# Attention backward for one query row: the score and grad products with the query standing and the keys moving

## The chip, the cores and the metric

The kernel runs on one core of a Trainium2 chip. The metric is device time in microseconds for one launch, the median of several runs. TensorE multiplies matrices (one operand stands in its array, the other moves through it) and writes PSUM; VectorE and ScalarE read and write PSUM and SBUF; SyncE and ScalarE issue the DMAs here. In the profile these are PE (PEld for its weight loads), DVE, ACT and SP.

## What is computed

For 2 x 32 = 64 heads, each with one query row of 128 and 8192 keys and values of 128, all in bf16: the output of softmax attention and the gradients of q, k and v for a given `grad_out`.

```python
def _fwd_reference(q, k, v):
    scale = q.shape[-1] ** -0.5
    scores = jnp.einsum("bhqd,bhkd->bhqk", q, k) * scale
    p = _softmax(scores, axis=-1)
    return jnp.einsum("bhqk,bhkd->bhqd", p, v)

def reference(q, k, v, grad_out):
    ...
    _out, _vjp = jax.vjp(_f, q, k, v)
    _grads = _vjp(grad_out)
    ...
```

With P = softmax(scale q k^T), dP = grad_out v^T and delta = sum(P dP): out = P v; dS = P (dP - delta); dq = scale dS k; dk is the outer product of scale dS and q; dv that of P and grad_out. Each head reads 4 MB (k, v) and writes 4 MB (dk, dv).

## The kernel before

A head's k is one SBUF tile `kt` of 128 partitions x 64 rows x 128 elements, its v another, `vt`; each is one DMA of 2 MB (`load`, L96). There are five buffers of each (`UNITS`). The gradients dv and dk are written in place over `vt` and `kt` and stored from there by ScalarE's queue (`store`, L277), so a load of head h+3 waits until the store of head h-2 has landed.

Scores and dP need k and v with the 128 elements on the partitions. A head is cut into eight steps j, four over k and four over v, each of two halves u of eight 128x128 blocks. `transposes` (L105) turns the eight blocks on TensorE by matmuls against the identity into `tp`, a PSUM tile of two banks of which there are two; ScalarE copies it to `ev` as bf16, VectorE does so for u=1 of j=0 and j=7 (L116). One half-step later in each group, `products` (L123) multiplies the blocks of the step before: each transposed block stands, and one column, q or grad_out of the head, moves, so that each block of 128 keys gives one column of 128 in `sm` (scores) or `dp`. Of step j=7, products follow in the next head's j=0.

Softmax for head h, called y in the loop, follows in its own pass: `row_max` (VectorE) after j=4, `all_max` at j=5 (a transpose on TensorE, then VectorE's `gm`), `exps` at j=6 (a matmul that spreads the maximum, VectorE's `negm`, ScalarE's exponential to `E`), and `to_weights` at the end of j=7, which puts E as bf16 columns into `wz`, the zero-padded weights of `weighted_rows`. The rest of a head p = h-1, called x, runs in the next head's pass: `deltas` (VectorE) after j=0, `sums` (TensorE) at j=1, `weights` (seven small VectorE instructions) after j=1, `weighted_rows` in j=0 to 3 (four concurrent matmuls with 32 standing columns and 512 moving each: out at j=0 and 1, dq at 2 and 3), eight `outer` products on VectorE in j=1 to 6, the store of v after j=4 and of k after j=7. Every fourth head the accumulator is copied out (`acc_to_sbuf`, after j=4) and `combine` (after j=6) picks four heads' rows into columns by f32 matmuls in a PSUM tile `c`; `spread_rows` copies q and grad_out of four heads to all partitions after j=7.

The order is written out by hand: `tc.manual_schedule()` (L298) keeps each engine's instructions in the order in which the loop emits them, and an engine that waits holds all behind it. So TensorE's order within a half-step is transposes, then what stands under `u == 0`, then products, then weighted rows; VectorE's and ScalarE's follow from the calls behind them.

[...]

Of the kernel before, what the change touches and what calls it, by code (L numbers as in the profile page):

```python
# [22 lines left out]
def kernel(  # L23
# [34 lines left out]
    for g in range(1, 4):  # L58
        nc.vector.tensor_add(out=pick[:], in0=pick[:], in1=idv[:, g])

    q_rows = q.rearrange("b h s d -> (b h s) d")
    do_rows = grad_out.rearrange("b h s d -> (b h s) d")
    o_rows = out_0.rearrange("b h s d -> (b h s) d")
# [16 lines left out]
    qT_all = const.tile([P, BH], BF16)  # L80
    doT_all = const.tile([P, BH], BF16)


    rl_all = const.tile([P, 2, BH], F32)
# [20 lines left out]
    def transposes(h, j, u):  # L105
# [14 lines left out]
        x.ev = getattr(x, "ev", {})  # L120
        x.ev[j, u] = ev

    def products(h, j, u):  # L123
        x = heads[h]
        w, c = divmod(j, NS // 2)
        if c == 0 and u == 0:
            if w:
                x.dp = ps_one.tile([P, NT + 2], F32, name="dp", tag="dp")
            else:
                x.sm = ps_one.tile([P, NT + P + 1], F32, name="sm", tag="sm")  # L130
        ev = x.ev.pop((j, u))
        col = (qT_all, doT_all)[w][:, h : h + 1]
        for i in range(HC):
            n = c * CH + u * HC + i
            nc.tensor.matmul(  # L135
                (x.dp if w else x.sm)[:, n : n + 1], lhsT=ev[:, i, :], rhs=col,
                start=True, stop=True,
            )

    def spread_rows(g):  # L140

# [14 lines left out]

    def row_max(x):
        x.mp = work.tile([P, 1], F32, name="mp", tag="mp")
        nc.vector.reduce_max(out=x.mp[:], in_=x.sm[:, 0:NT], axis=AX.X)  # L159

    def all_max(x):
        mT = x.sm[0:1, NT : NT + P]
        nc.tensor.transpose(mT, x.mp[:], ident_f[:])  # L163
        x.gm = work.tile([1, 1], F32, name="gm", tag="gm")
        nc.vector.reduce_max(out=x.gm[:], in_=mT, axis=AX.X)

    def exps(x):
        mb = x.sm[:, NT + P : NT + P + 1]
        nc.tensor.matmul(mb, lhsT=ones_f[0:1, :], rhs=x.gm[:], start=True, stop=True)  # L169
        negm = work.tile([P, 1], F32, name="negm", tag="negm")  # L170
        nc.vector.tensor_scalar(out=negm[:], in0=mb, scalar1=-scale, scalar2=None, op0=ALU.mult)  # L171
        x.E = work.tile([P, NT], F32, name="E_f", tag="E_f")
        x.ld = work.tile([P, 2], F32, name="ld", tag="ld")
        nc.scalar.activation(  # L174
            out=x.E[:],
            in_=x.sm[:, 0:NT],
            func=ACT.Exp,
            bias=negm[:],
            scale=scale,
            accum_out=x.ld[:, 0:1],  # L180
        )
# [8 lines left out]
    def deltas(x):  # L190
        junk = work.tile([P, NT], BF16, name="junk", tag="junk")
        nc.vector.tensor_tensor_reduce(  # L192
            out=junk[:],
            in0=x.E[:],
            in1=x.dp[:, 0:NT],
            scale=1.0,
            scalar=0.0,
            op0=ALU.mult,
            op1=ALU.add,
            accum_out=x.ld[:, 1:2],  # L200
        )

    def sums(x):
        x.lsum = x.dp[:, NT : NT + 2]
        nc.tensor.matmul(x.lsum, lhsT=ones_f[:], rhs=x.ld[:], start=True, stop=True)  # L205

    def weights(h):
        x = heads[h]
        rl, rls = rl_all[:, 0, h : h + 1], rl_all[:, 1, h : h + 1]
        nc.vector.reciprocal(out=rl, in_=x.lsum[:, 0:1])  # L210
        negdelta = work.tile([P, 1], F32, name="negdelta", tag="negdelta")
        nc.vector.tensor_scalar(
            out=negdelta[:], in0=x.lsum[:, 1:2], scalar1=rl, scalar2=-1.0,
            op0=ALU.mult, op1=ALU.mult,
        )
        nc.vector.tensor_scalar(out=rls, in0=rl, scalar1=scale, scalar2=None, op0=ALU.mult)
        dSu = work.tile([P, NT], F32, name="dSu", tag="dSu")
        nc.vector.scalar_tensor_tensor(
            out=dSu[:], in0=x.dp[:, 0:NT], scalar=negdelta[:], in1=x.E[:],
            op0=ALU.add, op1=ALU.mult,  # L220
        )
# [31 lines left out]
    def combine(h):  # L253

        x = heads[h]
        c = ps_one.tile([P, 2, OG], F32, name="c", tag="c")
        for j in range(4):
            nc.tensor.matmul(  # L258
                c[:], lhsT=x.accsb[:, j * D : (j + 1) * D], rhs=pick[:, j],
                start=(j == 0), stop=(j == 3),  # L260
            )
        own = slice(h - OG + 1, h + 1)
        nc.vector.tensor_mul(out=colsT[:, :, own], in0=c[:], in1=rl_all[:, :, own])
# [26 lines left out]
    for w in range(2):  # L290
        for t in wz[w]:
            nc.gpsimd.memset(t[:], 0.0)
    for src, dst in ((nat[:, 0, :], qT_all), (nat[:, 1, :], doT_all)):
        tps = ps_tp.tile([P, BH], BF16, name="tps", tag="tp")
        nc.tensor.transpose(tps[:], src, ident_bf[:BH, :BH])
        nc.vector.tensor_copy(out=dst[:], in_=tps[:])

    with tc.manual_schedule():  # L298
        for h in range(min(UNITS, BH)):
            load(h)  # L300
        for h in range(BH + 1):
# [4 lines left out]
            for j in range(NS):  # L306
                for u in range(2):
                    if y:
                        transposes(h, j, u)
                    if u == 0:  # L310
                        if x and j == 1:
                            sums(x)
                        if y and j == 5:
                            all_max(y)
                        if y and j == 6:
                            exps(y)
                    if y and j:
                        products(h, j - 1, u)
                    elif x and j == 0:
                        products(p, NS - 1, u)  # L320
                    if x and j < 4:
                        weighted_rows(p, j // 2, (2 * (j % 2) + u,))
                if x and j == 0:
                    deltas(x)
                if x and j == 1:
                    weights(p)
                if y and j == 4:
                    row_max(y)
                if y and j == 7:
# [51 lines left out]
```

## Time and profile before

| what | value |
|---|---|
| median of three runs | 1304.23 us (1302.53 to 1307.31) |
| the profiled execution | 1302.89 us |
| its span in the profile | 1301.1 us |
| mean granted TensorE clock | 0.885 |
| busy PE, PEld, DVE, ACT | 85%, 70%, 68%, 70% of the span |
| HBM traffic | 413 GB/s over the span |
| L135, all old products | PE busy 178.9 + 178.6 us, x8192; weight loads 332.4 us |
| L240, weighted rows | PE busy 124.3 + 108.2 us, x2048; mean of one 476 and 415 ns |
| L258, combine's matmuls, 128x128 standing, 8 moving, f32 | x128, 264 ns mean of one |
| L119, ScalarE's copy of `tp` | x896, 1025 ns |
| L270, outer products on VectorE | x512, 1212 and 1216 ns |
| L251, VectorE's copy 128x512 f32 from PSUM | x16, 683 ns |

Busy time of a group is the union of its instructions, so four concurrent matmuls of 415 ns count once. Where instructions of one engine overlap at their ends, the spacing of starts is shorter than the duration of one: four outer products in a row took 4.62 us.

### The profile page before, as it was taken

Reading aid. Unit: us, or ns where it says so; the run is one execution under the profiler, and the core shown is the slowest. Engines: PE = TensorE matmul, PEld = TensorE weight load, DVE = VectorE, ACT = ScalarE, POOL = GpSimd, SP = SyncE. Lnnn points to the kernel's source line nnn. Section 1 sums busy time; section 2 is a strip of 40 time slices with the busy share of each in tenths; the row PEclk is TensorE's granted clock in tenths of the full one; section 3 lists DMA queues with packets and bytes.
Section 4 is the critical chain, followed back from the end, with each engine's and each line's share of the span. In section 5 each row is a group of like instructions: output and inputs, shape, how many; then the busy total and the mean of one; then the engine's idle time right before and its main releaser. Section 6 shows DMA issues by size and latency. Waiting matters only on the chain.

```text
span 1301.1 us, 42243 instructions
## 1 busy us (share of the span) xinstructions
PE 1108.2 (85%) x18948; PEld 911.0 (70%) x18948; DVE 887.4 (68%) x1511; ACT 906.3 (70%) x1043; POOL 4.8 (0%) x16
## 2 busy tenths in 40 slices
PE   5999998988889879898898888988889888888784
PEld 5777777766767667677776767767767677677673
DVE  2887777766766767667676676766667667676566
ACT  5887778867767767676776766766668576676562
POOL 1000000000000000000000000000000000000000
PEclk9999989889887998888898888888899888898786
DMA  9999999999999999999999999999999999999986
GB/s 396 418 427 427 426 428 426 428 427 429 427 428 426 426 419 421 421 427 421 418 421 421 426 421 418 421 408 421 416 418 417 411 425 419 413 412 421 391 356 268
DMA packets 37653, 539.65 MB, mean 415 GB/s; under 512 B 4448, under 2 KB 4448, under 8 KB 4448
## 3 DMA queue, kind: packets, MB, share of 16 engines
q1 hardware_dynamic: 18432, 268.44, 49.6%
q10 hardware_dynamic: 19040, 268.51, 48.7%
q8 instruction: 148, 2.42, 0.7%
q14 instruction: 33, 0.27, 0.1%
HBM read 268.47 MB, written 268.47 MB: 413 GB/s over the span
## 4 chain that ended last, share of the span: by engine, by line
DMA 76%; PE 10%; ACT 6%; issue 4%; DVE 3%; ACTq 0%; DVEq 0%; SPq 0%
DMA out_dram<-kt 74%; PE tp L112 6%; ACT ev L119 5%; DVE ev L117 2%; PE acc L240 2%; DMA kt<-in_k_dram 1%; PE sm L135 1%; DMA nat<-in_grad_out_dram 1%; PE dp L205 0%; DVE kt L270 0%; DVE vt L270 0%; PE dp L135 0%; ACT E_f L174 0%; PE c L258 0%; PE sm L163 0%
## 5 line engine op out<-in xcount | busy, mean ns | idle before, releaser
L119 ACT CAST ev<-tp 128x1024 bf16<-128x1024 f32 x896 | 879.8, 1025 | 326.7 <-PE tp L112 270.7
L112 PE MATMUL tp<-ident_bf,kt 128*128 128x128 bf16 x4096 | 375.8, 245 | 83.3 <-DMA kt<-in_k_dram 54.8
L112 PEld LDWEIGHTS <-kt 128*128 128x128 bf16 x4096 | 281.1, 110 | 218.0 <-issue 156.4
L112 PE MATMUL tp<-ident_bf,vt 128*128 128x128 bf16 x4096 | 316.7, 221 | 60.4 <-ACT ev L119 44.3
L135 PEld LDWEIGHTS <-ev 128*128 128x128 bf16 x8192 | 332.4, 100 | 2.1 <-issue 0.2
L112 PEld LDWEIGHTS <-vt 128*128 128x128 bf16 x4096 | 260.9, 98 | 94.6 <-issue 74.2
L117 DVE CAST ev<-tp 128x1024 bf16<-128x1024 f32 x128 | 156.7, 1224 | 246.0 <-PE tp L112 237.3
L270 DVE TENSOR_TENSOR kt<-qd,dS 128x2048 bf16<-128x2048 bf16 x256 | 310.0, 1212 | 0.0
L270 DVE TENSOR_TENSOR vt<-qd,P 128x2048 bf16<-128x2048 bf16 x256 | 295.8, 1216 | 0.0
L135 PE MATMUL dp<-doT_all,ev 128*128 128x1 bf16 x4096 | 178.9, 165 | 0.1
L135 PE MATMUL sm<-qT_all,ev 128*128 128x1 bf16 x4096 | 178.6, 164 | 0.0
L240 PE MATMUL acc<-vt,wz 128*32 128x512 bf16 x1024 | 124.3, 476 | 9.3 <-DVE wz L185 9.2
L240 PE MATMUL acc<-kt,wz 128*32 128x512 bf16 x1024 | 108.2, 415 | 0.4 <-DVE wz L185 0.4
L240 PEld LDWEIGHTS <-wz 128*32 128x32 bf16 x2048 | 53.6, 95 | 21.7 <-DVE wz L185 12.4
L159 DVE TENSOR_REDUCE mp<-sm 128x1 f32<-128x64 f32 x64 | 14.4, 225 | 74.3 <-PE sm L135 74.3
L153 ACT CAST qd<-pb 128x1024 bf16<-128x1024 f32 x16 | 16.2, 1012 | 43.4 <-DMA out_dram<-kt 39.6
L210 DVE RECIPROCAL rl_all<-dp 128x1 f32<-128x1 f32 x64 | 10.8, 168 | 39.6 <-PE dp L205 39.6
L205 PE MATMUL dp<-ld,ones_f 128*128 128x2 f32 x128 | 28.4, 291 | 8.8 <-DVE ld L192 8.6
L205 PEld LDWEIGHTS dp<-ld,ones_f 128*128 128x128 f32 x128 | 24.8, 242 | 14.1 <-DVE ld L192 13.5
L171 DVE TENSOR_SCALAR negm<-sm 128x1 f32<-128x1 f32 x64 | 9.9, 154 | 23.9 <-PE sm L169 23.9
L169 PE MATMUL sm<-gm,ones_f 1*128 1x1 f32 x128 | 24.4, 257 | 0.0
L169 PEld LDWEIGHTS sm<-gm,ones_f 1*128 1x128 f32 x128 | 18.9, 184 | 6.7 <-issue 0.2
(40 smaller groups left out, 277.4 us busy)
## 6 DMA issues: line engine op xcount, KB each, us to landing
kt<-in_k_dram SPq DMA_DIRECT2D x64, 2048.0 KB, 18.9
vt<-in_v_dram SPq DMA_DIRECT2D x64, 2048.0 KB, 28.5
out_dram<-vt ACTq DMA_DIRECT2D x63, 2048.0 KB, 38.2
out_dram<-kt ACTq DMA_DIRECT2D x63, 2048.0 KB, 40.3
out_dram<-vt ACTq DMA_DIRECT2D x2, 1024.0 KB, 8.4
out_dram<-kt ACTq DMA_DIRECT2D x2, 1024.0 KB, 8.5
out_dram<-rows ACTq DMA_DIRECT2D x2, 16.0 KB, 7.4
nat<-in_q_dram ACTq DMA_DIRECT2D x1, 16.0 KB, 8.2
```

What stands on the lines that cost most here:

```text
L112: nc.tensor.matmul(tp[:, i, :], lhsT=x.kv[w][:, n, :], rhs=ident_bf[:], start=True, stop=True)
L117: nc.vector.tensor_copy(out=ev[:], in_=tp[:])
L119: nc.scalar.copy(out=ev[:], in_=tp[:])
L135: nc.tensor.matmul((x.dp if w else x.sm)[:, n : n + 1], lhsT=ev[:, i, :], rhs=col, start=True, stop=True,)
L153: nc.scalar.copy(out=qd[:], in_=pb[:])
L159: nc.vector.reduce_max(out=x.mp[:], in_=x.sm[:, 0:NT], axis=AX.X)
L169: nc.tensor.matmul(mb, lhsT=ones_f[0:1, :], rhs=x.gm[:], start=True, stop=True)
L171: nc.vector.tensor_scalar(out=negm[:], in0=mb, scalar1=-scale, scalar2=None, op0=ALU.mult)
L205: nc.tensor.matmul(x.lsum, lhsT=ones_f[:], rhs=x.ld[:], start=True, stop=True)
L210: nc.vector.reciprocal(out=rl, in_=x.lsum[:, 0:1])
L240: nc.tensor.matmul(acc[32 * g : 32 * g + 32, :], lhsT=wz[w][k][:, n // 4, :], rhs=rows[:, n : n + 4, :].rearrange("p n d -> p (n d)"), sta ...
L270: nc.vector.tensor_tensor(out=x.kv[1 - w][:, n : n + CH, :].rearrange("p n (d t) -> p n d t", t=2), in0=row.unsqueeze(1).to_broadcast([P, ...
```

## The change

The roles in `products` are exchanged. The head's column of q (or grad_out) stands, in the middle of a tile `qz` of 63 columns that are zero otherwise; a slice of 32 of its columns puts it at place c of 32 for chunk c. Four transposed blocks move at once, 512 columns, on the column tile 32g. Each half-step has two such matmuls, and four chunks accumulate into a PSUM tile `sT0` or `sT1`, where the score of a key then stands in row 32g + c. `rows_to_sbuf` copies that tile to SBUF as f32 (by VectorE for scores, by ScalarE for dP), and `rows_to_columns` brings it into columns with four f32 matmuls against `pick_m`, a matrix with one 1 in each of its 16 columns. The columns are in another order, so E, `deltas` and `dSu` read them through a reordered view. [...]

The loop gives the new steps places and moves others: the rows of dP are copied after j=0 and picked at j=1, `deltas` comes after j=1, `sums` at j=2, `weights` after j=2; `weighted_rows` runs in j = 0, 1, 3 and 4; scores are copied after j=4 and picked at j=5, `row_max` comes after j=5, `all_max` at j=6, `exps` at j=7. The outer products stand in pairs in j=3 to 6, the store of v after j=5; `acc_to_sbuf` after j=5, `combine` after j=7. `set_columns` fills the next head's `qz` after j=2.

```diff
+    pick_m = const.tile([P, CH], F32)
+    idg = ident_f[:].rearrange("p (g r) -> p g r", g=4)[:, :, 0:4]
+    nc.vector.tensor_copy(
+        out=pick_m[:].rearrange("p (c g) -> p c g", g=4), in_=idg.rearrange("p g c -> p c g")
+    )
...
+    qz = [const.tile([P, 2, 63], BF16, name=f"qz{i}") for i in range(2)]
...
+    def set_columns(h):
+        nc.vector.tensor_copy(out=qz[h % 2][:, :, 31], in_=qdT_all[:, :, h])
...
         ev = x.ev.pop((j, u))
-        col = (qT_all, doT_all)[w][:, h : h + 1]
-        for i in range(HC):
-            n = c * CH + u * HC + i
+        for i in range(2):
+            g = 2 * u + i
             nc.tensor.matmul(
-                (x.dp if w else x.sm)[:, n : n + 1], lhsT=ev[:, i, :], rhs=col,
+                x.sT[w][32 * g : 32 * g + 32, :],
+                lhsT=qz[h % 2][:, w, 31 - c : 63 - c],
+                rhs=ev[:, 4 * i : 4 * i + 4, :].rearrange("p n d -> p (n d)"),
+                start=(c == 0),
+                stop=(c == NT // CH - 1),
+                tile_position=(0, 32 * g),
+            )
+
+    def rows_to_sbuf(x, w):
+        x.sTsb = work.tile([P, 4 * P], F32, name="sTsb", tag="sTsb")
+        if w:
+            nc.scalar.copy(out=x.sTsb[:], in_=x.sT[w][:])
+        else:
+            nc.vector.tensor_copy(out=x.sTsb[:], in_=x.sT[w][:])
+
+    def rows_to_columns(x, w):
+
+        t = (x.sm, x.dp)[w]
+        for b in range(4):
+            nc.tensor.matmul(
+                t[:, b * CH : (b + 1) * CH], lhsT=x.sTsb[:, b * P : (b + 1) * P], rhs=pick_m[:],
                 start=True, stop=True,
             )
+
+    def in_order(t):
+        return t.rearrange("p (b m) -> p m b", b=4)
...
-        c = ps_one.tile([P, 2, OG], F32, name="c", tag="c")
+        c = ps_tp.tile([P, 2, OG], F32, name="c", tag="tp")
...
                     if u == 0:
                         if x and j == 1:
+                            rows_to_columns(x, 1)
+                        if x and j == 2:
                             sums(x)
                         if y and j == 5:
+                            rows_to_columns(y, 0)
+                        if y and j == 6:
                             all_max(y)
-                        if y and j == 6:
+                        if y and j == 7:
                             exps(y)
...
-                    if x and j < 4:
-                        weighted_rows(p, j // 2, (2 * (j % 2) + u,))
+                    if x and j in (0, 1, 3, 4):
+                        weighted_rows(p, j // 3, (2 * (j - (0, 3)[j // 3]) + u,))
                 if x and j == 0:
+                    rows_to_sbuf(x, 1)
+                if x and j == 1:
                     deltas(x)
-                if x and j == 1:
+                if x and j == 2:
                     weights(p)
                 if y and j == 4:
+                    rows_to_sbuf(y, 0)
+                if y and j == 5:
                     row_max(y)
+                if j == 2 and h + 1 < BH:
+                    set_columns(h + 1)
                 if y and j == 7:
                     to_weights(h, 0, y.E)
-                if x and p < BH - 1 and j in (4, 7):
+                if x and p < BH - 1 and j in (5, 7):
                     store(p, j // 7)
                 if x:
-                    for i in ((), (0,), (1, 2), (3, 4), (5,), (6,), (7,), ())[j]:
+                    for i in ((), (), (), (0, 1), (2, 3), (4, 5), (6, 7), ())[j]:
                         outer_and_store(p, i // 4, i % 4)
-                    if full and j == 4:
+                    if full and j == 5:
                         acc_to_sbuf(x)
-                    if full and j == 6:
+                    if full and j == 7:
                         combine(p)
```

More of the change, by code (lines that the diff above doesn't have):

```diff
@@ L79 @@
     acc = ps_one.tile([P, 4 * D], F32, name="acc", tag="acc")
-    qT_all = const.tile([P, BH], BF16)
-    doT_all = const.tile([P, BH], BF16)
+    qdT_all = const.tile([P, 2, BH], BF16)
+    qz = [const.tile([P, 2, 63], BF16, name=f"qz{i}") for i in range(2)]
     rl_all = const.tile([P, 2, BH], F32)
@@ L126, in products @@
         if c == 0 and u == 0:
[L127 to L130, printed above, removed]
+            x.sT = getattr(x, "sT", [])
+            x.sT.append(ps_one.tile([P, 4 * P], F32, name=f"sT{w}", tag=f"sT{w}"))
+            if w == 0:
+                x.cols = ps_one.tile([P, 2 * NT + P + 3], F32, name="cols", tag="cols")
+                x.sm, x.dp = x.cols[:, 0:NT], x.cols[:, NT : 2 * NT]
+                x.mT = x.cols[0:1, 2 * NT : 2 * NT + P]
+                x.mb = x.cols[:, 2 * NT + P : 2 * NT + P + 1]
+                x.lsum = x.cols[:, 2 * NT + P + 1 : 2 * NT + P + 3]
         ev = x.ev.pop((j, u))
-        col = (qT_all, doT_all)[w][:, h : h + 1]
-        for i in range(HC):
-            n = c * CH + u * HC + i
+        for i in range(2):
+            g = 2 * u + i
             nc.tensor.matmul(
-                (x.dp if w else x.sm)[:, n : n + 1], lhsT=ev[:, i, :], rhs=col,
+                x.sT[w][32 * g : 32 * g + 32, :],
[16 more added lines that the diff above has]
+                t[:, b * CH : (b + 1) * CH], lhsT=x.sTsb[:, b * P : (b + 1) * P], rhs=pick_m[:],
                 start=True, stop=True,
             )
+    def in_order(t):
+        return t.rearrange("p (b m) -> p m b", b=4)
     def spread_rows(g):
@@ L158, in row_max @@
         x.mp = work.tile([P, 1], F32, name="mp", tag="mp")
-        nc.vector.reduce_max(out=x.mp[:], in_=x.sm[:, 0:NT], axis=AX.X)
+        nc.vector.reduce_max(out=x.mp[:], in_=x.sm, axis=AX.X)
     def all_max(x):
-        mT = x.sm[0:1, NT : NT + P]
-        nc.tensor.transpose(mT, x.mp[:], ident_f[:])
+        nc.tensor.transpose(x.mT, x.mp[:], ident_f[:])
         x.gm = work.tile([1, 1], F32, name="gm", tag="gm")
-        nc.vector.reduce_max(out=x.gm[:], in_=mT, axis=AX.X)
+        nc.vector.reduce_max(out=x.gm[:], in_=x.mT, axis=AX.X)
     def exps(x):
-        mb = x.sm[:, NT + P : NT + P + 1]
-        nc.tensor.matmul(mb, lhsT=ones_f[0:1, :], rhs=x.gm[:], start=True, stop=True)
+        nc.tensor.matmul(x.mb, lhsT=ones_f[0:1, :], rhs=x.gm[:], start=True, stop=True)
         negm = work.tile([P, 1], F32, name="negm", tag="negm")
-        nc.vector.tensor_scalar(out=negm[:], in0=mb, scalar1=-scale, scalar2=None, op0=ALU.mult)
+        nc.vector.tensor_scalar(out=negm[:], in0=x.mb, scalar1=-scale, scalar2=None, op0=ALU.mult)
         x.E = work.tile([P, NT], F32, name="E_f", tag="E_f")
@@ L174, in exps @@
         nc.scalar.activation(
-            out=x.E[:],
-            in_=x.sm[:, 0:NT],
+            out=x.E[:].rearrange("p (m b) -> p m b", b=4),
+            in_=in_order(x.sm),
             func=ACT.Exp,
@@ L192, in deltas @@
         nc.vector.tensor_tensor_reduce(
-            out=junk[:],
-            in0=x.E[:],
-            in1=x.dp[:, 0:NT],
+            out=junk[:].rearrange("p (m b) -> p m b", b=4),
+            in0=x.E[:].rearrange("p (m b) -> p m b", b=4),
+            in1=in_order(x.dp),
             scale=1.0,
@@ L203, in sums @@
     def sums(x):
-        x.lsum = x.dp[:, NT : NT + 2]
         nc.tensor.matmul(x.lsum, lhsT=ones_f[:], rhs=x.ld[:], start=True, stop=True)
@@ L218, in weights @@
         nc.vector.scalar_tensor_tensor(
-            out=dSu[:], in0=x.dp[:, 0:NT], scalar=negdelta[:], in1=x.E[:],
+            out=dSu[:].rearrange("p (m b) -> p m b", b=4), in0=in_order(x.dp), scalar=negdelta[:],
+            in1=x.E[:].rearrange("p (m b) -> p m b", b=4),
             op0=ALU.add, op1=ALU.mult,
@@ L292 @@
             nc.gpsimd.memset(t[:], 0.0)
-    for src, dst in ((nat[:, 0, :], qT_all), (nat[:, 1, :], doT_all)):
+    for src, dst in ((nat[:, 0, :], qdT_all[:, 0]), (nat[:, 1, :], qdT_all[:, 1])):
         tps = ps_tp.tile([P, BH], BF16, name="tps", tag="tp")
         nc.tensor.transpose(tps[:], src, ident_bf[:BH, :BH])
-        nc.vector.tensor_copy(out=dst[:], in_=tps[:])
+        nc.vector.tensor_copy(out=dst, in_=tps[:])
+    for t in qz:
+        nc.vector.memset(t[:], 0.0)
+    set_columns(0)
     with tc.manual_schedule():
```

## The prediction

> **What bounds the kernel now.** I read the page's head and its chain first, then the engines' timelines of one head, then the granted clock in short windows.
>
> The page (span, two rows over 40 slices, the chain by engine):
>
> ```profile
> span 1301.1 us, 42243 instructions
> ...
> DMA  9999999999999999999999999999999999999986
> GB/s 396 418 427 427 426 428 426 428 427 429 427 428 426 426 419 421 421 427 421 418 421 421 426 421 418 421 408 421 416 418 417 411 425 419 413 412 421 391 356 268
> ...
> DMA 76%; PE 10%; ACT 6%; issue 4%; DVE 3%; ACTq 0%; DVEq 0%; SPq 0%
> ```
>
> The DMA engines are full until the last two slices, and the chain is 76% DMA: one head (4 MB in, 4 MB out) every 20.25 us or so (the k loads are issued at 1153.10, 1173.34, 1193.67 and 1213.90). Compute is only just behind that. At full clock one head takes 17.3 us: the same v store is issued at 183.18 and 200.32, the same reduction starts at 183.20 and 200.35. But the granted clock is 0.885 in the mean, and the list of waits has TensorE waiting for a k landing only 54.8 us in all. So a change that costs compute over 3 us a head takes the bound from DMA.
>
> VectorE at the end of a head (start, duration, instruction; an idle time and its releaser in brackets):
>
> ```profile
> 183.20 0.23 DVE L159 TENSOR_REDUCE mp<-sm 128x1 f32<-128x64 f32 x1 [0.52 <-PE sm L135]
> 183.34 1.22 DVE L270 TENSOR_TENSOR kt<-qd,dS 128x2048 bf16<-128x2048 bf16 x1
> 184.47 0.27 DVE L165 TENSOR_REDUCE gm<-sm 1x1 f32<-1x128 f32 x1
> 184.68 1.20 DVE L270 TENSOR_TENSOR kt<-qd,dS 128x2048 bf16<-128x2048 bf16 x1
> 186.08 0.16 DVE L171 TENSOR_SCALAR negm<-sm 128x1 f32<-128x1 f32 x1 [0.20 <-PE sm L169]
> 186.16 1.22 DVE L270 TENSOR_TENSOR kt<-qd,dS 128x2048 bf16<-128x2048 bf16 x1
> 188.87 1.23 DVE L117 CAST ev<-tp 128x1024 bf16<-128x1024 f32 x1 [1.50 <-PE tp L112]
> 190.01 0.18 DVE L185 CAST wz<-E_f 128x64 bf16<-128x64 f32 x1
> ```
>
> From the finished scores (183.2) to the weights wz that TensorE waits for at 190.2, three outer products stand in VectorE's order, and it idles 1.5 us before ev: there the loop is TensorE's.
>
> One TensorE step at half and at full clock (transposes, products, weighted rows, next transposes):
>
> ```profile
> 283.48 1.03 PE L112 MATMUL tp<-ident_bf,kt 128*128 128x128 bf16 x8
> 284.30 0.40 PE L135 MATMUL dp<-doT_all,ev 128*128 128x1 bf16 x8
> 284.63 0.62 PE L240 MATMUL acc<-vt,wz 128*32 128x512 bf16 x4
> 285.18 1.03 PE L112 MATMUL tp<-ident_bf,kt 128*128 128x128 bf16 x8
> ```
> ```profile
> 190.58 0.62 PE L112 MATMUL tp<-ident_bf,kt 128*128 128x128 bf16 x8
> 191.04 0.34 PE L135 MATMUL dp<-doT_all,ev 128*128 128x1 bf16 x8
> 191.31 0.40 PE L240 MATMUL acc<-vt,wz 128*32 128x512 bf16 x4
> 191.65 0.62 PE L112 MATMUL tp<-ident_bf,kt 128*128 128x128 bf16 x8
> ```
>
> By starts, eight transposes take 0.46 us, eight products 0.27, four weighted rows 0.33 at full clock; 0.82, 0.33 and 0.55 at half.
>
> The clock in windows of 3.41 us, the step in which it changes (columns here: length, busy and count of the transposes and their weight loads, clock, DMA share, GB/s):
>
> ```profile
> 164.61:168.03 3.42, 1.72 (x26) 1.42 (x24) 1.00 1.00 426
> 168.03:171.44 3.41, 1.97 (x19) 1.56 (x17) 0.50 1.03 437
> 171.44:174.85 3.41, 2.07 (x18) 1.54 (x17) 0.50 0.99 423
> 174.85:178.26 3.41, 1.70 (x23) 1.18 (x22) 1.00 0.98 413
> ```
>
> The clock is 1 or 0.5. I counted, for each such window, the moving columns of the matmuls that start in it, times the share of the 128x128 array they use (a transpose 128, a weighted-row matmul 128, an old product 1). Of 287 windows at full clock, the 253 followed by full clock hold 3,088 or more (one 2,960), and the 34 followed by half clock 2,904 or less (two 3,092 and 3,094). At half clock it is the same: 33 recover, with 3,084 or more but for one, and 51 of the 55 that stay hold 2,964 or less. So a window needs some 3,050 columns, or the next runs at half clock, whether TensorE was idle in it or not. The first window above holds 2,906 (the combine's small f32 matmuls stand in it).
>
> **The change, part by part.** Call T the start of a head's second group of transposes (step j=0, u=1).
>
> Products: eight loads and one-column matmuls become two 512-column ones on two column tiles. The nearest row is the weighted rows: four such, concurrent, 0.33 us. Bounds: 0.17 (half of the group) and 0.45 (one, mean 415 to 476 ns, with no overlap of the two). I take 0.30, near the group, since each streams the same 512 columns: nothing gained on 0.27. Sixteen groups a head at the bounds: -2 to +2.5 us. In windows they count 256 instead of 8.
>
> [...]
>
> Copy of the rows: on ScalarE for grad_out, 128x512 f32: between 0.36 (128x64, L174) and 1.03 (128x1024, L119), by elements 0.66. On VectorE 0.68 (L251, same shape), 0.65 with overlap.
>
> Picking into columns: four f32 matmuls, eight instructions; L258 has this stationary shape with 8 columns: 0.90 us for eight at full clock (96.89, next at 97.79), 1.88 near half (1289.29). Taken 0.95 and 1.8, twice a head.
>
> Stage one, T to the scores in VectorE's reach: nine steps of 0.46+0.30 = 6.84; six of them with weighted rows, 1.98; the sums 0.24; the first picking 0.95 and 0.1 of waiting for ScalarE's copy (0.76+0.2+0.66 after T against TensorE's 1.55); 0.2 for the result to reach VectorE: 10.3 us. VectorE's weights (1.27), the column copy (about 0.15) and outers 0 and 1 (2.31) end by T+9: hidden.
>
> Stage two is new. VectorE's order is now: copy of the scores, outers 2 and 3, row maximum, outers 4 and 5, gm, outers 6 and 7, negm, ev, wz: 0.65 + 6 x 1.155 + 0.14 + 0.21 + 0.08 + 1.14 + 0.18, and 0.06 + 0.33 for the first weighted rows that wait for wz: 9.7 us. The steps that are picked, transposed and evacuated meanwhile are ready earlier. Behind the waiting weighted rows stands all of TensorE: the next T. Together 20.0 us against 17.3.
>
> Every fourth head: acc_to_sbuf (0.62) stands before gm, and c and pb both take a tp buffer, so the next transposes wait for VectorE's product and ScalarE's copy: about 1.75 us, 0.44 a head. Period 20.45 at full clock.
>
> The clock: between the transposes of (7,0), done by T+15.1, and the weighted rows at T+19.7 TensorE has two groups of transposes and three of products: 2 x 1,024 + 3 x 256 = 2,816 in 4.6 us. A window inside has too few, as have those that begin from T+15.0 to T+18.05: nine heads in ten meet one. The half clock then falls on stage one, where a step is 0.82+0.50+0.55 and the picking 1.8 us with next to nothing counted, so one or two more windows stay under. Stepped through at three positions (0.7, -1.6, -0.8 us from T) the clock is back after 2, 3 and 4 windows, and stage one is 2.9, 3.8 and 5.6 us longer; I take 4.0, times 0.9: 3.6. Period 24.05.
>
> [...]
>
> At nothing: qz, pick_m and the first column copies (while the rows of q and grad_out land, until 11.8; else about 1 us once); the reordered reads of E and dp (off VectorE's and ScalarE's loop by 0.4 us; else some 0.1 each); the v store a step later (no DMA is waited for while a head takes over 20.25 us; else about 2 us once); a later E (ready 0.4 us before ev ends).
>
> Edges: T of head 1 at about 30; after the last T the 23.3 us from 1277.8 to the end, and 2 for copy and picking. 55 + 63 x 24.05 = **1570 us**. The profiled execution took 1302.89, 1.3 below the median.
>
> **Rivals.** (a) The longer loop with the clock mostly full: 55 + 63 x 20.45 = 1343; with a dip in every third head 55 + 63 x 21.8 = 1428. It decides where the 4.6 us poor in columns are under a window, 3.41. For it: the margin is 1.2 us. Against: from gm to wz alone, two outers, negm, ev and wz make 3.7 us. (b) The DMA hides it: if stage one is shorter by my bound of 0.13 x 9 and the half clock absent, the period is 19.3, under 20.25: 1301, within 6. (c) Faster: the added columns (4,096 for 128 a head) end the dips after 1220, where compute is the chain and the clock is 0.76 and 0.83 in two stretches of 20 us: 0.24 x 20 + 0.17 x 20 = 8 us, so 1293. It needs a period under 17.5 us, so stage two 2.5 us shorter than VectorE's order makes it. (d) The two product matmuls don't overlap: 0.15 x 9 more at full, twice that at half clock: 1655 to 1700.
>
> **How the numbers follow.** Forecast 0.66 (own range 1480 to 1650), (a) 0.20, (b) 0.05, (c) 0.06, (d) 0.03. Under 0.5%, 6.5 us, this kernel's times can't be told from no change. Faster 0.06, same 0.05, slower 0.89. The range 1340 to 1650 leaves out (b), (c) and (d), 0.14.
>
> **What would show it.** Right: TensorE waits at the weighted rows for wz about once a head, over 1 us; VectorE has no idle time from the scores' copy to wz; clock near 0.8 (nine microseconds of 24 at half); half-clock windows begin around each head's first weighted rows; DMA at eight tenths, hardly a wait for k. Wrong: a DMA row of nines (b), a clock above 0.9 (a), VectorE idle before ev (c), 0.45 us between a product group and what follows (d).

## The result, and the profile after

The changed kernel takes 1370.49 us (median of 4 runs, 1370.01 to 1370.97) beside 1304.88 for the kernel before on the same chip: a ratio of 1.0504, interval 1.0485 to 1.0523. It is slower, as forecast, but by 66 us and not by 266.

The page of the changed kernel, the rows shown of before (span, DMA share and GB/s in 40 slices, the chain by engine):

```profile
span 1368.2 us, 32135 instructions
...
DMA  9999999999999999999999999999999999999966
GB/s 397 378 378 391 385 414 394 409 391 412 422 380 417 403 399 423 366 428 395 404 402 388 423 397 407 397 393 422 400 407 394 394 423 385 419 391 403 419 262 248
...
PE 51%; DVE 26%; DMA 18%; issue 5%; ACT 0%; ACTq 0%; DVEq 0%
```

The chain has gone from 76% DMA to TensorE and VectorE. The DMA row is still a row of nines, which I had named as a sign that the DMA hides the change. It isn't: the rate fell from 413 to 392 GB/s, the store of dk lands after 16.7 us where before it took 40.3, and TensorE's waits for a k landing, 54.8 us before, are 0.2 us, of its weight loads. The share of busy time of the DMA engines says little here; the time to landing says it.

VectorE at the end of one head (start, duration, instruction; idle time and releaser in brackets):

```profile
630.28 0.69 DVE L165 COPY sTsb<-sT 128x512 f32<-128x512 f32 x1 [1.66 <-PE sT L151]
630.89 2.35 DVE L307 TENSOR_TENSOR vt<-qd,P 128x2048 bf16<-128x2048 bf16 x2
633.16 0.22 DVE L198 TENSOR_REDUCE mp<-cols 128x1 f32<-128x64 f32 x1
633.29 2.35 DVE L307 TENSOR_TENSOR kt<-qd,dS 128x2048 bf16<-128x2048 bf16 x2
635.56 0.27 DVE L203 TENSOR_REDUCE gm<-cols 1x1 f32<-1x128 f32 x1
635.76 2.34 DVE L307 TENSOR_TENSOR kt<-qd,dS 128x2048 bf16<-128x2048 bf16 x2
638.03 0.14 DVE L208 TENSOR_SCALAR negm<-cols 128x1 f32<-128x1 f32 x1
638.10 1.20 DVE L125 CAST ev<-tp 128x1024 bf16<-128x1024 f32 x1
639.23 0.17 DVE L222 CAST wz<-E_f 128x64 bf16<-128x64 f32 x1
```

From the copy of the scores to wz VectorE has no idle time: this is the stage two of the prediction, instruction by instruction. TensorE's list of waits shows the other end of it, 1.1 us at the first weighted rows of every head but each fourth one (waited for: us in total, times, longest):

```profile
PE acc L277 <- DVE wz L222: 55.4, 49, 1.9
PE cols L206 <- DVE gm L203: 20.0, 62, 0.8
```

Now the clock. It changes in steps of 3.41 us here too: the changed kernel's stretches at half clock, but for the last, which runs to the end, are 3.41, 6.83 and 10.24 us long. Four windows of one step, two pairs of neighbours (columns: length; busy time and count of PE, PEld, DVE, ACT, POOL; clock, DMA share, GB/s):

```profile
613.71:617.13 3.42, 2.52 (x24) 1.88 (x22) 3.17 (x6) 0.41 (x2) 0.00 (x0) 1.00 1.02 422
617.13:620.54 3.41, 3.41 (x29) 1.81 (x28) 0.17 (x1) 2.02 (x2) 0.00 (x0) 0.50 1.04 387
740.01:743.42 3.41, 2.42 (x24) 1.45 (x24) 3.41 (x5) 1.97 (x5) 0.00 (x0) 1.00 1.13 389
743.42:746.83 3.41, 3.28 (x40) 2.20 (x40) 1.52 (x4) 1.98 (x3) 0.00 (x0) 1.00 0.95 298
```

TensorE is busy for 2.52 us in the first window, and the clock halves behind it; it is busy for only 2.42 in the third, and the clock stays. So busy time doesn't decide. What the two windows hold (TensorE's timeline):

```profile
613.60 0.39 PE L151 MATMUL sT<-ev,qz 128*32 128x512 bf16 x2
613.92 0.62 PE L120 MATMUL tp<-ident_bf,vt 128*128 128x128 bf16 x8
614.47 0.39 PE L151 MATMUL sT<-ev,qz 128*32 128x512 bf16 x2
614.80 1.06 PE L295 MATMUL c<-pick,accsb 128*128 128x8 f32 x8
616.76 0.67 PE L184 MATMUL pb<-nat,ident_bf 64*128 64x256 bf16 x4 [0.90 <-DVE ev L125]
...
740.29 0.39 PE L151 MATMUL sT<-ev,qz 128*32 128x512 bf16 x2
740.61 0.62 PE L120 MATMUL tp<-ident_bf,vt 128*128 128x128 bf16 x8
741.16 0.39 PE L151 MATMUL sT<-ev,qz 128*32 128x512 bf16 x2
741.49 0.62 PE L120 MATMUL tp<-ident_bf,kt 128*128 128x128 bf16 x8
742.04 0.39 PE L151 MATMUL sT<-ev,qz 128*32 128x512 bf16 x2
```

The third window holds two groups of transposes and three product pairs. That is the poor stretch of the prediction, 2 x 1,024 + 3 x 256 = 2,816 columns in the prediction's count, under its bound of 3,050. The clock doesn't fall. The mean clock is 0.965, where I had expected 0.8.

### The profile page after: what moved, and what is told of

It is laid out like the page before. It is cut to its first block, busy times and chain, and to the rows that moved or that the text cites. A ratio compares the mean times of both kernels' runs of the same rounds, so it can differ in the third digit from the quotient of the medians.

```text
span 1368.2 us, 32135 instructions
## 1 busy us (share of the span) xinstructions
PE 1252.4 (92%) x13828; PEld 775.4 (57%) x13828; DVE 925.1 (68%) x1642; ACT 964.1 (70%) x1107; POOL 4.8 (0%) x16
## 3 DMA queue, kind: packets, MB, share of 16 engines
q8 instruction: 108, 1.77, 0.5%
## 4 chain that ended last, share of the span: by engine, by line
PE 51%; DVE 26%; DMA 18%; issue 5%; ACT 0%; ACTq 0%; DVEq 0%
PE tp L120 24%; DMA out_dram<-kt 15%; PE sT L151 14%; DVE kt L307 12%; PE acc L277 6%; DVE vt L307 4%; DVE ev L125 4%; PE cols L171 4%; DVE sTsb L165 2%; DMA kt<-in_k_dram 2%; PE cols L206 1%; DVE mp L198 1%; PE pb L184 1%; DVE gm L203 1%; DMA nat<-in_grad_out_dram 1%
## 5 line engine op out<-in xcount | busy, mean ns | idle before, releaser
L151 PE MATMUL sT<-ev,qz 128*32 128x512 bf16 x2048 | 409.7, 397 | 0.0
L120 PEld LDWEIGHTS <-kt 128*128 128x128 bf16 x4096 | 244.4, 101 | 183.7 <-issue 183.4
L120 PE MATMUL tp<-ident_bf,kt 128*128 128x128 bf16 x4096 | 335.3, 228 | 1.9 <-DVE ev L125 1.8
L120 PEld LDWEIGHTS <-vt 128*128 128x128 bf16 x4096 | 230.3, 98 | 153.8 <-issue 152.4
L277 PE MATMUL acc<-kt,wz 128*32 128x512 bf16 x1024 | 153.0, 388 | 1.1 <-DVE wz L222 1.1
L151 PEld LDWEIGHTS <-qz 128*32 128x32 bf16 x2048 | 98.7, 93 | 92.4 <-issue 17.2
L171 PE MATMUL cols<-pick_m,sTsb 128*128 128x16 f32 x1024 | 137.9, 267 | 1.9 <-ACT sTsb L163 0.5
L171 PEld LDWEIGHTS cols<-pick_m,sTsb 128*128 128x128 f32 x1024 | 126.2, 194 | 18.2 <-DVE sTsb L165 12.6
L165 DVE COPY sTsb<-sT 128x512 f32<-128x512 f32 x64 | 44.3, 692 | 114.1 <-PE sT L151 114.1
L163 ACT COPY sTsb<-sT 128x512 f32<-128x512 f32 x64 | 37.4, 585 | 71.1 <-PE sT L151 71.1
## 6 DMA issues: line engine op xcount, KB each, us to landing
vt<-in_v_dram SPq DMA_DIRECT2D x64, 2048.0 KB, 21.3
out_dram<-vt ACTq DMA_DIRECT2D x63, 2048.0 KB, 12.2
out_dram<-kt ACTq DMA_DIRECT2D x63, 2048.0 KB, 16.7
```

Of the source, the lines that this page charges most:

```text
L120: nc.tensor.matmul(tp[:, i, :], lhsT=x.kv[w][:, n, :], rhs=ident_bf[:], start=True, stop=True)
L151: nc.tensor.matmul(x.sT[w][32 * g : 32 * g + 32, :], lhsT=qz[h % 2][:, w, 31 - c : 63 - c], rhs=ev[:, 4 * i : 4 * i + 4, :].rearrange("p n ...
L163: nc.scalar.copy(out=x.sTsb[:], in_=x.sT[w][:])
L165: nc.vector.tensor_copy(out=x.sTsb[:], in_=x.sT[w][:])
L171: nc.tensor.matmul(t[:, b * CH : (b + 1) * CH], lhsT=x.sTsb[:, b * P : (b + 1) * P], rhs=pick_m[:], start=True, stop=True,)
L277: nc.tensor.matmul(acc[32 * g : 32 * g + 32, :], lhsT=wz[w][k][:, n // 4, :], rhs=rows[:, n : n + 4, :].rearrange("p n d -> p (n d)"), sta ...
```

## The experiments

All spacings below are from one row maximum (line 198 of the changed kernel) to the next. In the changed kernel they are 19.95 us where nothing disturbs, 23.1 to 24.3 in the head after every fourth (the first such 26.2; these are the "fourth heads" below), and 20.88 in the mean of 63, with 52.6 us of edges. Two theories stood at the start: that VectorE's order sets the undisturbed head, and that the prediction's clock count was wrong in its unit. Diffs are against the changed kernel unless said otherwise; three dots stand for lines left out.

**One outer product earlier.** Is it VectorE's order, or TensorE's own work?

```diff
-                    for i in ((), (), (), (0, 1), (2, 3), (4, 5), (6, 7), ())[j]:
+                    for i in ((), (), (0,), (1, 2), (3, 4), (5, 6), (7,), ())[j]:
```

> The changed kernel with one outer product moved out of the stretch between the scores' copy and wz (pairs become one after j=2, two after j=3, j=4 and j=5, one after j=6). Theory, VectorE's order sets the loop: the spacing of the scores' copies in undisturbed heads falls from 19.95 us by one outer product, 1.16, to about 18.8, which is under the DMA's 20.25, so the DMA takes over: 1298 to 1312 us. Rival, TensorE's work (92% busy) is the bound and VectorE only fills: 1365 to 1375 us.

Measured: 1301.04 us, ratio 0.9979 (0.9967 to 0.9991), clock 0.985; undisturbed heads 19.12, the fourth 20.96 (two of them, with half clock, 23.67 and 22.38). VectorE's timeline of this kernel, the end of a head:

```profile
635.01 0.69 DVE L165 COPY sTsb<-sT 128x512 f32<-128x512 f32 x1 [0.53 <-PE sT L151]
...
641.63 0.14 DVE L208 TENSOR_SCALAR negm<-cols 128x1 f32<-128x1 f32 x1
641.98 1.23 DVE L125 CAST ev<-tp 128x1024 bf16<-128x1024 f32 x1 [0.21 <-PE tp L120]
```

One outer fewer behind the scores gives 0.83 of its 1.155 us; the idle time ahead of the scores falls from 1.66 to 0.53, and VectorE now waits 0.21 us for TensorE's last transposes. So VectorE's order was the bound, and TensorE is some 0.2 us behind it. Of the 69 us less, 63 x 0.83 = 52 are this shorter head; the rest goes with less half clock, 24 us of the loop instead of 78. The time lies in the expected range, but not because the DMA took over: the chain is 53% TensorE, 30% VectorE and 13% DMA.

**Half the columns.** The products move 256 columns instead of 512, so the windows stream less.

```diff
-                x.sT[w][32 * g : 32 * g + 32, :],
+                x.sT[w][32 * g : 32 * g + 32, 0 : 2 * P],
...
-                rhs=ev[:, 4 * i : 4 * i + 4, :].rearrange("p n d -> p (n d)"),
+                rhs=ev[:, 4 * i : 4 * i + 2, :].rearrange("p n d -> p (n d)"),
...
```

> The changed kernel whose products move 256 of each 512 columns; the copies take the same half twice, so half of the keys' scores and dP are replaced by the other half's, and the picking is as long as before. Theory, a window's clock goes by the time in which the array streams (a pair of products 512 columns, now 256): between the transposes of (7,0) and the weighted rows stand 2 x 1,024 + 3 x 256 = 2,816 columns, under some 3,070, so most heads get windows at half clock: mean clock 0.75 to 0.88, 1400 to 1530 us, slower with less work. [...]

Measured: 1395.29 us, 1.0705 (1.0676 to 1.0734), clock 0.89. Undisturbed heads are shorter, 18.93, but many have a stretch at half clock and take 20.4 to 23.0, the fourth 24.9 to 26.3. TensorE's timeline where the first such stretch begins:

```profile
51.15 0.62 PE L279 MATMUL acc<-vt,wz 128*32 128x512 bf16 x4 [1.43 <-DVE wz L224]
51.70 1.03 PE L120 MATMUL tp<-ident_bf,kt 128*128 128x128 bf16 x8
```

Eight transposes take 1.03 us from there on. It is the place where the prediction put the fall, at a head's first weighted rows: with half as many columns it comes about there in 23 ordinary heads and in all 15 fourth ones, 283 us of the loop or 4.5 a head (the forecast for all the columns had nine), and less work takes longer. Direction as expected, size a little under the range.

**The order alone.** The new order of steps with the old products; no copies, no picking.

```diff
-        for i in range(2):
-            g = 2 * u + i
+        for i in range(HC):
+            n = c * CH + u * HC + i
             nc.tensor.matmul(
-                x.sT[w][32 * g : 32 * g + 32, :],
...
+                (x.dp if w else x.sm)[:, n : n + 1], lhsT=ev[:, i, :],
+                rhs=qdT_all[:, w, h : h + 1], start=True, stop=True,
```

> The changed kernel's order of steps with the old products (a transposed block stands, one column moves), so without copies and picking. Theory, VectorE's order and the streaming clock: without the clock the period would be 9.0 + 9.05 = 18.1 us, under the DMA's 20.25; but between the transposes of (7,0) and the weighted rows only 2,072 columns stream, so each head meets a window at half clock, stage one is 3 to 5 us longer, 21 to 23 us a head: 1370 to 1480 us, mean clock 0.75 to 0.85. Rival, the clock doesn't go by streamed columns, or the copies and picking are what costs: DMA-bound, 1300 to 1310 us.

Measured: 1306.39 us, 1.0017 (1.0007 to 1.0027), clock 0.864, undisturbed heads 16.46, and the chain is 80% DMA. The expectation missed by far; the rival's range was hit, with the DMA as the bound. VectorE's timeline says why:

```profile
636.67 4.62 DVE L303 TENSOR_TENSOR vt<-qd,P 128x2048 bf16<-128x2048 bf16 x4
641.21 0.22 DVE L194 TENSOR_REDUCE mp<-sm 128x1 f32<-128x64 f32 x1
```

With no copy in VectorE's order, outers 0 to 3 run ahead of the row maximum without a pause and only four stand behind it. In the changed kernel the copy holds outers 2 and 3 back, and VectorE idles before it. From the row maximum to wz both kernels take 6.07 us; the 3.49 us between 16.46 and 19.95 lie ahead of it: from T, as the prediction has it, to the row maximum it is 9.83 and 13.33. There the changed kernel has the later scores, with a picking and longer products before them, and then the copy and two outers, 2.88 us. By themselves the moved steps cost nothing here, under the DMA's bound; which share is the scores' lateness and which the copy's place, this run doesn't separate.

**The scores copied by ScalarE.** Then is the copy's place the cause?

```diff
-        if w:
-            nc.scalar.copy(out=x.sTsb[:], in_=x.sT[w][:])
-        else:
-            nc.vector.tensor_copy(out=x.sTsb[:], in_=x.sT[w][:])
+        nc.scalar.copy(out=x.sTsb[:], in_=x.sT[w][:])
```

> The changed kernel with the scores' copy on ScalarE, so that outers 2 and 3 no longer stand behind it on VectorE. Theory, the whole way from scores to row maximum counts (copy, picking, row maximum), not only the copy's place: ScalarE has an evacuation before it, the copy ends about 1.45 us after the scores, the picking at 2.5, the row maximum starts at 2.65 where it started at 2.9; the idle time moves to the front of the row maximum, the spacing in undisturbed heads stays at 19.7 to 19.95 us, the time at 1355 to 1372. Rival, the copy's place in VectorE's order is the whole loss: spacing 18 us or less, 1300 to 1315 us.

Measured: 1328.46 us (1321.88 and 1335.05), 1.0189 (1.0144 to 1.0235), clock 0.982; undisturbed heads 19.46, fourth heads 21.3 to 22.7. Neither number was hit. VectorE's timeline:

```profile
644.92 4.63 DVE L304 TENSOR_TENSOR vt<-qd,P 128x2048 bf16<-128x2048 bf16 x4
651.32 0.23 DVE L195 TENSOR_REDUCE mp<-cols 128x1 f32<-128x64 f32 x1 [1.77 <-PE cols L168]
```

Outers 2 and 3 now run early, but VectorE idles 1.77 us before the row maximum: copy and picking still stand between the products and the scores, and make them late. Only 0.49 us of a head comes from the copy's engine.

**The fourth heads.** Three edits took parts of what stands there. First `combine` and `spread_rows` after j=6, away from the head's boundary:

```diff
-                    if full and j == 7:
+                    if h == BH and j == 7:
                         combine(p)
+                    if h >= 2 and (h - 2) % OG == OG - 1 and j == 6:
+                        combine(h - 2)
+                if j == 6 and y and h % QG == 0:
+                    spread_rows(h // QG)
...
-                    if y and h % QG == 0:
-                        spread_rows(h // QG)
```

> The changed kernel with combine moved to after j=6 of the next head's pass and spread_rows to after j=6, so that neither takes a tp buffer at the end of j=7 of every fourth head. Theory, those heads' 23.2 to 24.3 us against 19.95 come from the two waits for tp and the half clock that follows: they fall to 20.6 to 21, the mean to 20.1 to 20.3, and the time to 1318 to 1335 us with a clock over 0.98. Rival, it is the accumulator's copy before gm and the windows at half clock come anyway: 1355 to 1370 us.

Measured: 1381.46 us, 1.0599 (1.0583 to 1.0615), slower than the change itself and than both expected ranges. The head with `spread_rows` falls to 20.55, but that with `combine` now takes 22.9 to 24.5. TensorE's list of waits:

```profile
PE tp L120 <- DVE colsT L300: 31.2, 15, 2.1
```

Fifteen times TensorE waits some 2.1 us for VectorE to read `c`, in a stretch that was poor already, and half clock follows.

Then `c` in spare columns of `cols`, the tile of the scores' and dP's columns, so that it holds no `tp` buffer, and `spread_rows` after j=6:

```diff
-        c = ps_tp.tile([P, 2, OG], F32, name="c", tag="tp")
+        c = (heads[h + 1] if h + 1 < BH else x).cols[:, 2 * NT + P + 3 :].rearrange("p (w k) -> p w k", w=2)
...
```

> The changed kernel with combine at its place but writing spare columns of the bank of cols, not a tp buffer, and spread_rows after j=6. Theory, the wait of transposes for a tp buffer and the half clock after it make the fourth heads dear, not combine itself: they fall from 23.2 to 24.3 us to about 20.6 (the accumulator's copy remains), the mean to 20.1, the time to 1316 to 1330 us, clock over 0.98. Rival, combine's f32 matmuls themselves starve the clock: 1355 to 1372 us.

Measured: 1360.26 us (1352.54 to 1367.68), 1.0414 (1.0369 to 1.0459). Fourth heads take 21.4 without half clock and 22.8 to 27.3 with it. The new place has a wait of its own (TensorE's weight loads, list of waits):

```profile
PEld cols L295 <- ACT E_f L211: 21.7, 15, 1.5
```

`cols` is also what ScalarE reads for E, so the combine waits for that. The time is in the rival's range; whether its reason holds, the next run tells.

Last, no `combine` but for the last group:

```diff
-                    if full and j == 7:
+                    if h == BH and j == 7:
                         combine(p)
...
```

> The changed kernel without combine for all groups of four heads but the last (out and dq of the others are left zero); spread_rows and the accumulator's copy stay. Theory, combine is what makes the fourth heads dear: its f32 matmuls stream almost nothing in the poorest stretch, and c holds a tp buffer until VectorE comes to it: 23.2 to 24.3 us become 20.6 to 21.5, the clock 0.98 or more, the time 1318 to 1335 us. Rival, spread_rows' wait for a tp buffer brings the half clock by itself: 1350 to 1370 us.

Measured: 1375.20 us, 1.0541 (1.0525 to 1.0556), no faster than with it; fourth heads take 22.4 or 25.2 to 25.3. TensorE's timeline in a fourth head (`pb` is the tile that `spread_rows` fills):

```profile
699.45 0.61 PE L185 MATMUL pb<-nat,ident_bf 64*128 64x256 bf16 x4
701.41 1.01 PE L121 MATMUL tp<-ident_bf,kt 128*128 128x128 bf16 x8 [1.35 <-DVE ev L126]
```

`spread_rows` alone holds a `tp` buffer long enough: TensorE waits 1.35 us for VectorE to empty the other one, and goes on at half clock. So `combine` is not the cause by itself, and the rival's reason is what the row shows, with a time 5 us over its range.

**Useless work as a test of the clock.** If the clock goes by what streams, matmuls that nobody needs must raise it. First in the kernel with the order alone: one 512-column matmul on one column tile behind each product group, into a PSUM tile of its own.

```diff
+        nc.tensor.matmul(
+            fill[0:32, :], lhsT=ident_bf[:, 0:32], rhs=ev[:, 0:4, :].rearrange("p n d -> p (n d)"),
+            start=True, stop=True, tile_position=(0, 0),
+        )
...
```

> The order alone (old products), with one useless matmul added behind each group of products: 32 standing columns, 512 moving, into a spare bank that nobody reads. It does no work for the result. Theory, the clock goes by the time in which anything streams: a filler counts 512, the poor stretch before the weighted rows goes from 2,072 columns to 3,608, so the windows at half clock go: mean clock from 0.864 to 0.96 or more, spacing in undisturbed heads from 16.46 to 18.2 to 18.8 us, and the time stays with the DMA, 1294 to 1306 us. Rival, what counts is the share of the array that works: a filler counts 128, the stretch has 2,456, clock 0.82 to 0.90 as before, and the longer steps with three or four microseconds of half clock pass the DMA: 1320 to 1400 us.

Measured: 1317.45 us, 1.0102 (1.0085 to 1.0119); the clock is 0.988 where the same kernel without it had 0.864. The time missed its range, since each filler takes 0.33 us of TensorE and the undisturbed head becomes 19.38; the clock did what the theory said. By the prediction's unit, in which a filler counts 128 columns, windows of down to 2,116 columns stay at full clock here.

Then in the fourth heads of the changed kernel, where the half clock falls: 15 transposes of the identity ahead of `combine`. Written to spare columns of `cols`:

```diff
...
+                        if y:
+                            for _ in range(15):
+                                nc.tensor.matmul(y.fill, lhsT=ident_bf[:], rhs=ident_bf[:], start=True, stop=True)
                         combine(p)
```

> The changed kernel with fifteen useless transposes of the identity (1,920 columns, about 0.85 us) in front of combine in every fourth head, into spare columns of cols that nobody reads; TensorE waits there for VectorE anyway. Theory, the half clock makes most of the fourth heads' excess: with the columns added the windows at half clock go, clock 0.985 or more, fourth heads fall from 23.6 us in the mean to 21.4 to 22.2 (the prediction's price without the clock was 20.0 + 1.75), the time from 1370 to 1330 to 1348 us. Rival, the excess is the waits for tp and the f32 matmuls, and the clock dips are a symptom: 1365 to 1380 us, since TensorE has more to do.

Measured: 1410.60 us, 1.0796 (1.0771 to 1.0822), clock 0.942. TensorE's timeline:

```profile
112.81 1.76 PE L392 MATMUL cols<-ident_bf 128*128 128x128 bf16 x15 [1.20 <-ACT E_f L212]
```

The filler itself waited 1.20 us for ScalarE's read of `cols`, and so lengthened the poor stretch: half clock for 17.1 us in six of the fifteen fourth heads, which then take 30 us. As a test it is inconclusive; it shows what a wait at this place costs.

Written to the tile of the scores instead, which is free by then:

```diff
-                                nc.tensor.matmul(y.fill, lhsT=ident_bf[:], rhs=ident_bf[:], start=True, stop=True)
+                                nc.tensor.matmul(
+                                    y.sT[0][:, 0:P], lhsT=ident_bf[:], rhs=ident_bf[:], start=True, stop=True
+                                )
```

> The fifteen useless transposes again, now into sT0, which has been copied out by then, so that they wait for nobody (in cols they waited 1.20 us for ScalarE's E and lengthened the poor stretch). Theory, the half clock makes most of the fourth heads' excess: clock 0.985 or more, fourth heads from 23.6 us in the mean to 21.4 to 22.2, the time from 1370 to 1330 to 1348 us. Rival, the waits and the f32 matmuls are the excess: 1365 to 1380 us.

Measured: 1339.38 us (1339.08 to 1339.49), 1.0276 (1.0259 to 1.0293), clock 0.993. Ordinary heads stay at 19.95, and the 15 fourth heads take 21.79 each. TensorE's timelines of a fourth head, first of the changed kernel, then of this one:

```profile
697.52 0.39 PE L151 MATMUL sT<-ev,qz 128*32 128x512 bf16 x2
697.84 1.06 PE L295 MATMUL c<-pick,accsb 128*128 128x8 f32 x8
699.80 1.01 PE L184 MATMUL pb<-nat,ident_bf 64*128 64x256 bf16 x4 [0.90 <-DVE ev L125]
700.74 1.03 PE L120 MATMUL tp<-ident_bf,kt 128*128 128x128 bf16 x8
```
```profile
600.52 0.39 PE L151 MATMUL sT<-ev,qz 128*32 128x512 bf16 x2
600.85 1.01 PE L391 MATMUL sT<-ident_bf 128*128 128x128 bf16 x15
601.70 1.01 PE L295 MATMUL c<-pick,accsb 128*128 128x8 f32 x8
602.81 0.59 PE L184 MATMUL pb<-nat,ident_bf 64*128 64x256 bf16 x4
603.33 0.62 PE L120 MATMUL tp<-ident_bf,kt 128*128 128x128 bf16 x8
```

The filler's 0.85 us stand where TensorE waited 0.90 us anyway, and `pb` and the transposes behind it run at full clock. 15 x 15 useless matmuls take 31 us off.

**The parts together.** Two kernels tried to beat the kernel before: all of it moved (`c` in `cols`, `spread_rows` after j=6, both copies on ScalarE, outers from j=2), and one outer earlier with `c` in `cols` and `spread_rows` after j=6. The lines of the first that no earlier diff shows:

```diff
...
-                    for i in ((), (), (), (0, 1), (2, 3), (4, 5), (6, 7), ())[j]:
+                    for i in ((), (), (0, 1), (2, 3), (4,), (5, 6), (7,), ())[j]:
```

> The previous run's edit together with the scores' copy on ScalarE and the outer products at two after j=2, two after j=3, one after j=4, two after j=5, one after j=6: the idle time before the row maximum is filled. Theory: 18.6 to 18.9 us in undisturbed heads, under the DMA's 20.25 us, so the DMA sets the time and only the tail can gain, where full clock shortens the last heads: 1285 to 1300 us. Rival, TensorE's longer products and pickings keep the loop above the DMA's: 1310 us and more.

> One outer product earlier, combine in cols, spread_rows after j=6. Theory: 19.1 us in undisturbed heads and 19.8 in fourth ones, both under the DMA's 20.25: DMA-bound with a clock of 0.98 or more, 1288 to 1300 us, at or below the run with one outer product earlier alone (1301.04). Rival, that run was already bound by the DMA throughout: 1299 to 1303 us.

Measured: 1302.85 us, 0.9990 (0.9980 to 1.0000), and 1301.80, 0.9980 (0.9969 to 0.9991). Both lie just over the expected ranges; the second is in its rival's. The chains by engine, of the first and of the second:

```profile
PE 78%; ACT 10%; DVE 5%; DMA 5%; issue 1%; ACTq 0%; DVEq 0%; SPq 0%
```
```profile
DMA 43%; PE 38%; DVE 14%; ACT 2%; issue 2%; ACTq 0%; DVEq 0%; SPq 0%
```

The first is bound by TensorE's own work at 19.41 us a head. The second begins at 19.12 and 20.28, but many of its last 25 heads take 19.8 to 21.6 and its dk stores 35.0 us to land: there the DMA is the bound again, as before the change. No variant is faster than the kernel before by more than 0.21%, less than the 0.5% under which the prediction counts times as the same.

## Why the direction was right and the size wrong

**Stage one and two: right.** Predicted 10.3 + 9.7 = 20.0 us at full clock. Measured 10.45 (next transposes at 639.78, copy of the next scores at 650.23) and 9.50, together 19.95. The first experiment shows that stage two is what VectorE's order makes it, as the prediction said. Single terms: picking 0.99 us for 0.95, 1.8 at half clock as taken; ScalarE's copy 0.585 for 0.66; a step with weighted rows 1.09 for 1.09; one without 0.87 for 0.76. The last was under-sized by 0.11: the pair takes 0.33 to the next transposes, not 0.30, and it begins 0.55 us after the transposes where an old product began 0.46 after. What the 0.09 us are, no run here shows. Three such steps make 0.33 us and the sum of stage one is only 0.15 short, so other terms were over-sized by about as much: that the sum is so near is partly luck. Two numbers of the prediction are off and carry nothing: the bounds of the product term give 16 x (-0.10 to +0.18), which is -1.6 to +2.9 us a head and not -2 to +2.5, and the rows beside "one head takes 17.3 us" give 17.15 (most undisturbed heads of before take 17.29).

**Edges: right.** 55 predicted, 52.6 measured.

**Every fourth head without the clock: right.** Predicted 1.75 us, 0.44 a head. With the filler the fourth heads are 21.79, 1.84 over the others, and the mean spacing 20.40 is 0.45 over 19.95. The whole sum without its clock term, 55 + 63 x 20.45 = 1343, meets the 1339.38 of that kernel within 0.3%.

**The clock: the step that failed.** "In windows they count 256 instead of 8", and from it "2 x 1,024 + 3 x 256 = 2,816 in 4.6 us. A window inside has too few" and "the clock is back after 2, 3 and 4 windows": 3.6 us a head, 63 x 3.6 = 227 us. Measured it is 20.88 - 20.40 = 0.48 a head, the 31 us that the filler took away, and only in the fourth heads: 78 us of the loop run at half clock, none of them in an ordinary head. This term is nearly the whole error: 63 x (3.6 - 0.48) = 197 of the 199.5 us that were too many.

Its mistake is the unit. I weighted each matmul by its share of the array, 32 of 128 columns. The rows of before allowed that: its only matmuls of 32 columns came four at once, and 4 x 128 are the same 512 as the time in which any of them streams. The change has two at once, where share says 256 and streaming time 512. Counted by streaming time, in columns, the window from 740.01 holds 2 x 1,024 + 3 x 512 = 3,584, and that from 613.71 some 2,730. The runs, all windows at full clock, sorted by the clock of the next (a matmul is spread over the windows in which it streams, so the figures of before differ by a little from those of the prediction; by how the ends are spread, all are good to some 50):

| kernel | next full, lowest by share | next full, lowest by time | next half, most by time |
|---|---|---|---|
| before | 3,088 | 3,099 | 2,920 |
| changed | 2,594 | 2,999 | 2,781 |
| half the columns | 2,543 | 2,950 | 3,152 |
| order alone with filler | 2,116 | 3,154 | 2,932 |

("Next half" leaves out three windows of before at 3,104 to 3,136, one of the changed kernel at 3,444 and two of the last at 3,456 and 3,575, which this count doesn't explain.) By share the bound would have to move from 3,088 to 2,116 between kernels; by time it stays near 3,050, within 100 or so, with windows of the kernel with half the columns on both sides of it between 2,950 and 3,150. Windows at half clock go the same way but for some of the kernel with half the columns, up to 3,426 by time, and of the kernel with the filler in `cols`, up to 3,283, which don't recover.

The exceptions have something in common that the count by time leaves out. All six, and all those at half clock over 3,060 that don't recover, hold `pb`'s four matmuls, whose standing operand has 64 of 128 rows (64*128 in the lines). Counted at half, the six come to 2,592 to 2,624, 2,971, and 2,989 and 3,100, and no window at half clock stays there with more than 2,983. Of the 4,891 full-clock windows of all fourteen kernels, one bound chosen afterwards for each count misplaces 53 by share (the prediction's 3,050 would misplace 218), 49 by time alone, and 25 by time with half the rows at half (15 of these in the kernel with half the columns); of 490 at half clock 52, 35 and 10. So the share of columns was the wrong half of the prediction's unit; the share of rows fits, by the count alone, since no run varied it.

Halving the streamed columns brought the fall (clock 0.89 for 0.965), and adding useless ones took it away (0.988 for 0.864, 0.993 for 0.965). Whether the clock's own measure is time, or something that goes with it, no run here tells.

Idle time doesn't decide it either. The longest in the window from 613.71 is 0.90 us, and half clock follows; in the window from 740.01 TensorE stands still from 742.43 to the window's end, 0.99 us of the 1.11 us it waits for wz, and full clock follows.

**The rivals.** What happened is (a), the longer loop with the clock mostly full, 1343 to 1428, to which I gave 0.20. Its sign, a clock above 0.9, came. I had put its deciding point right (is the poor stretch under a window?) and answered it in the wrong unit. (b) needed a period under 20.25 us; the mean is 20.88. (c) needed a shorter stage two, which has the length of its sum. (d) is out: the pairs overlap, 0.33 us to the next group.

**At nothing.** The later v store, the reordered reads and the column copies cost nothing that the lists of waits show.

## What to carry to other kernels

Before a count from one kernel is carried over a change, look for the instructions on which two readings of it would differ; if the old kernel has none, both readings belong in the range, and the likelier can't be told from its fit. Where an engine's order is fixed, as here, a step that waits for another engine (the copy of the scores out of PSUM, with 1.66 us idle before it) sets the place of everything behind it: fill the time ahead of it first (one outer product moved there took 0.83 us off a head). Where TensorE waits in a stretch that is poor in columns, matmuls that nobody needs and that wait for nothing can be worth more than their time (0.85 us in every fourth head took 31 us off; the same matmuls behind a wait of 1.20 us put 40 us on).

## What the runs showed of the hardware that was not expected

- In these runs the granted clock goes with how long TensorE streams, rather than with how many of the array's columns are in use (windows of 2,116 columns by share stay at full clock with the filler, windows of 2,592 to 2,918 fall in the kernel before) or with the busy time of the profile: half clock after a window with 2.52 us busy and full clock after one with 2.42. f32 matmuls of 8 and 16 columns fill 0.9 to 1.06 us for eight instructions and are only 64 and 128 columns in this count: the window from 613.71 holds eight of the first kind, and half clock follows.
- Less work can be slower: half the columns, 1.0705 instead of 1.0504. More can be faster: 1339.38 us with the filler for 1370.49.
- The DMA engines show nine tenths and more at 392 GB/s with stores landing in 12.2 and 16.7 us, just as at 413 GB/s with 38.2 and 40.3: their busy share alone doesn't say that they are the bound.
